# Weight loads in quarters, x tiles ahead of wk, k projections begun by block, single products for the factors, and engine orders written out, in a gated mix of segment attention and a token MLP

## The chip, the cores and the metric

The kernel runs on one core of a Trainium2 chip. The metric is device time in microseconds: the time of one execution of the program. Before the change three runs gave 178.17, 178.38 and 179.44, median 178.38.

## What is computed

Two branches work on the same x (2048 tokens by 448 features), and a gate per token mixes them. Cut to what matters:

```python
g = sigmoid((x * gate_w).sum(-1))
# A: 16 heads of 28 features; the sequence is cut into 4 segments of 512 tokens
q, k, v = x @ wq, x @ wk, x @ wv
for s in range(4):
    p = softmax(q_s k_s^T * 28**-0.5 + causal mask)          # inside the segment
    a_mem = phi(q_s) M / (phi(q_s) z + 1e-6)                 # what earlier segments left
    out_s = sigmoid(beta) * a_mem + (1 - sigmoid(beta)) * (p v_s)
    M, z = M + phi(k_s)^T v_s, z + phi(k_s).sum()            # phi(t) = t + 1 if t > 0 else exp(t)
a = out @ wo
# B: an MLP over the tokens (2048 -> 1792 -> 2048) for each feature
b = (gelu(layernorm(x)^T w1 + b1) w2 + b2)^T
return g * a + (1 - g) * b
```

## The kernel before, in words

Everything is one basic block. Each piece of work is recorded by `op` (line 89) with its engine, what it reads and writes, and an estimated cost; `plan` (line 157) then puts the recorded operations into one fixed order for each engine, and `finalize` (line 280) works out the semaphore waits. On the chip each engine runs its own list from the top, and an operation that waits holds up all that stand behind it on its engine. `plan` before the change is a list scheduler: it advances estimated times, takes for each engine the ready operation of the lowest priority number, shifts that number by a table (`SHIFTS`, line 354), and gives out PSUM banks and buffers as they come free. Where an operation names an `alt` engine, `plan` chooses between the two.

The stages are these.

- **Loading.** x comes in as 16 natural tiles of 128 tokens (`load_x`, line 522, into `xh`), and a second time as transposed tiles `xT` by DMA transposes from DRAM (`transpose_x`, line 536) for segments 1 to 3. Segment 0 is transposed on TensorE (`transposes_0`, line 667, matmuls of line 675) out of the first four x tiles. wk, wq and wv come in by `load_w` (line 526); VectorE then copies wk and wq into a padded layout `wqk` with 32 columns a head (`pad_w`, line 648, copies of line 649).
- **Projections.** q and k of a segment are made feature-major, v token-major. The 448 input features are 3 blocks of 128 and a remainder of 64, so `pair` (line 694) does two projections together: the two remainders as two 64-row tiles that run side by side (named lo...), then three full matmuls for each projection (pr...). For segment 0 the k projections are made in halves of 256 tokens. The last 4 features of each head's 32 rows hold parts of further heads; they are gathered through DRAM (`gather`, lines 755 and 760, DMAs on SP) into head group 3.
- **Attention.** 16 units (4 segments by 4 head groups) make 8 pairs of 5 fills. For each fill `scores` (line 942) does 4 row-tiled matmul groups into PSUM banks 0 to 3 (line 954), ScalarE takes one exp over 128x2048 (line 963), and GpSimd masks (line 966). `pv_unit` (line 971) multiplies by v with column tiles of 32 (line 990) and, from segment 1 on, by the memory (named mem). VectorE then transposes both results in 32x32 blocks (lines 1004, 1006), makes reciprocals and scales (1015 to 1019), GpSimd adds (1021), and VectorE transposes back into `oT` (line 1027), which the output projection `wo_tile` (line 1033) reads; ScalarE or VectorE takes that out (lines 1047, 1051). `do_mst` (line 831) accumulates the memory; four small products of 32 rows each (line 860) put it with the factor `maskg` into a block-diagonal matrix.
- **MLP.** `mm1` (line 1055) makes 14 tiles of 16 matmuls, `mm2` (line 1082) 16 tiles of 14 matmuls; their weights come through a ring of three slots of 1 MB (`ring_load`, line 569), one DMA and one semaphore for a slot. ScalarE and VectorE share the gelu (lines 1065 to 1078). VectorE finishes an output tile (line 1093) and SP stores it (line 1097). The last tile is done in columns 0 to 320 and 320 to 448.

All matmuls that may use any layout go through `mm` (line 329, matmul of line 332): as one 128x128 matmul, or, when the run of full-height work around them holds column-tiled ones, as four of 32 columns. So the TensorE stream alternates between four tile shapes: 128x128, 64 rows (lo), 32 rows (scores) and 32 columns.

Names that the text uses: `trx0_0` and `trx0_1` are the transposes of x tiles 0, 1 and 2, 3; `lok0_0` is the first remainder pair; `ot15` is the last transpose into `oT`; the wo tiles 12 to 15 read what `ot12` to `ot15` wrote, and are followed by the four last output tiles of `mm2`.

Of the kernel before, what the change touches and what calls it, by code (L numbers as in the profile page):

```python
# [74 lines left out]
class Sched:  # L75
# [13 lines left out]
    def op(self, eng, fn, reads=(), writes=(), name=None, dma=False, out=False, cost=100.0, prio=0.0, mode="f",  # L89
           nbytes=0, rel=0.0, port=False, take=None, use=(), alt=None,  # L90
# [27 lines left out]
        if dma:  # L118
            self._dma_uid += 1
            o.evspace = "dma_u%d" % self._dma_uid  # L120
            o.is_event = True
# [35 lines left out]
    def plan(self, shifts=()):  # L157

        import bisect

        shifts = dict(shifts)
        for o in self.ops:
            o.prio = (o.prio[0] + shifts.get(o.name.split("-")[0], 0.0), o.idx)
        succ = [[] for _ in self.ops]
        left = [0] * len(self.ops)
        ready = [o.rel for o in self.ops]
        for o in self.ops:
            for d in {x.idx: x for x in o.deps + o.order}.values():
                succ[d.idx].append(o)
                left[o.idx] += 1  # L170
        free = {e: 0.0 for e in ENGINES}
        mode = "f"
        chan = 0.0
        port = 0.0
        waiting = {e: [] for e in ENGINES}
        avail = {e: [] for e in ENGINES}
        banks = {p: {b: (0.0, []) for b in v} for p, v in self.pool.items()}
        for p, v in self.later.items():
            banks[p].update({b: (1e18, []) for b in v})

        def push(o):
            for e in o.alts:
                bisect.insort(waiting[e], (ready[o.idx], o.prio, o))

        for o in self.ops:
            if left[o.idx] == 0:
                push(o)
        line = []
        while len(line) < len(self.ops):
            best = None  # L190
            for e in ENGINES:
                w, a = waiting[e], avail[e]
                t = free[e]
                while w and w[0][0] <= t:
                    _, p, o = w.pop(0)
                    if o.start is None:
                        bisect.insort(a, (p, o))
                a[:] = [x for x in a if x[1].start is None]
                w[:] = [x for x in w if x[2].start is None]
                while True:  # L200
                    pick = None
                    can = [o for p, o in sorted(a + [(x[1], x[2]) for x in w if x[0] <= t])
                           if not o.take or sum(v[0] <= t for v in banks[o.take[0].pool].values()) >= len(o.take)]
                    if can:
                        pick = can[0]
                        if e == "PE":

                            if mode != "f":
                                lead = [o.prio for o in can if o.tile == "f"][:1]
                                tiled = [o for o in can if o.tile == "r" or o.tile == "h" and ([o.prio] <= lead or not lead)]  # L210
                                tiled = [o for o in tiled if o.tile == mode] + tiled
                                pick = tiled[0] if tiled else pick
                            elif pick.tile == "h":
                                rest = [o for o in can if o.tile == "f"]
                                if rest and not any(o.tile == "r" for o in can) and t < ready[pick.idx] + pick.hold:
                                    pick = rest[0]
                        break
                    nxt = [x[0] for x in w if x[0] > t][:1]
                    if a or w:
                        nxt += [v[0] for p in banks.values() for v in p.values() if t < v[0] < 1e12]  # L220
                    if not nxt:
                        break
                    t = min(nxt)
                if pick is not None and (best is None or t < best[0]):
                    best = (t, e, pick)
            t, e, o = best
            for g in o.take:
                pool = banks[g.pool]
                b = min((v[0], b) for b, v in pool.items())[1]
                g.bank = b  # L230
                o.deps = o.deps + pool[b][1]
                pool[b] = (1e18, [])
            o.eng = e
            o.fn, c, pt = o.alts[e]
            if o.evspace is None:
                o.evspace = e
            if e == "PE" and t < COLD:
                c *= 2.0
            if e == "PE" and o.tile != mode:
                c += SWITCH  # L240
                mode = o.tile
            if pt:
                t = max(t, port)
                port = t + c
            o.start = t
            o.cost = c
            free[e] = t + c
            if o.nbytes:
# [12 lines left out]
            for x in succ[o.idx]:  # L261
# [5 lines left out]
                if left[x.idx] == 0:  # L267
                    push(x)
# [955 lines left out]
```

## Time and profile before

| what | value |
|---|---|
| runs | 178.17, 178.38, 179.44 us, median 178.38 |
| profiled execution | 178.57 us, its span 176.8 us (1.77 us lie around it) |
| TensorE (PE) busy | 169.7 us, 2354 matmul records |
| VectorE (DVE) busy | 149.6 us, 337 instructions |
| ScalarE (ACT) busy | 134.1 us, 170 instructions |
| GpSimd (POOL) busy | 69.2 us, 93 instructions |
| granted TensorE clock | 1.0 throughout |

The page gives busy times by engine, the span in 40 slices, and the chain of work that ended last, followed back from the last instruction. The other views cut out a window, list instructions in order of time, group them by shape, or give each engine's busy time in chosen stretches. Matmuls are pipelined, so the time between the starts of matmuls, and not the busy time of one, is what a matmul costs.

### The profile page before, as it was taken

What the parts mean: (1) busy time and instruction counts of PE and PEld (TensorE: products, weight loads), DVE (VectorE), ACT (ScalarE), POOL (GpSimd) and SP (SyncE); (2) the same over time, 40 slices, a digit from 0 to 9 for tenths busy, and PEclk for the clock granted to TensorE, in tenths of its full rate; (3) what the DMA queues carried; (4) which work ended last, traced back from release to release, by engine and by line L of the source; (5) the groups of instructions that cost most, each with busy time, mean ns of one, the idle gap of its engine ahead of it and who ended that gap; (6) DMA issues with size and microseconds to landing.
All of it is one profiled execution on the core that took longest, in us unless ns stands there. A gap on an engine that the chain in (4) does not pass through costs nothing.

```text
span 176.8 us, 5552 instructions
## 1 busy us (share of the span) xinstructions
PE 169.7 (96%) x2354; PEld 81.8 (46%) x2354; DVE 149.6 (85%) x337; ACT 134.1 (76%) x170; POOL 69.2 (39%) x93
## 2 busy tenths in 40 slices
PE   8699999999999999999999999999999999999993
PEld 3343443345544544444544344444444544555652
DVE  6499999799995898998999999997889999992222
ACT  2277898999689999999999999987878877405100
POOL 8003016542302233437745644359474425450000
PEclk9999999999999999999999999999999999999999
DMA  6979983699939915852007360203938600166511
GB/s 153 281 142 304 259 158 84 167 302 193 245 78 268 240 35 161 192 171 46 4 11 201 77 170 22 61 28 95 224 99 227 170 8 4 56 176 194 153 59 52
DMA packets 49752, 24.62 MB, mean 139 GB/s; under 512 B 14256, under 2 KB 49488, under 8 KB 49728
## 3 DMA queue, kind: packets, MB, share of 16 engines
q1 hardware_dynamic: 49440, 24.05, 56.6%
q8 instruction: 18, 0.29, 0.7%
q10 hardware_dynamic: 288, 0.23, 0.6%
q14 instruction: 6, 0.05, 0.1%
HBM read 18.76 MB, written 2.36 MB: 119 GB/s over the span
## 4 chain that ended last, share of the span: by engine, by line
PE 78%; ACT 6%; DVE 6%; DMA 4%; SPq 3%; issue 2%
PE t L332 67%; PE t L954 6%; PE t L990 4%; DMA t<-in_A_wk_dram 3%; ACT t L963 2%; SPq L760 1%; SPq L755 1%; DVE t L913 1%; PE t L840 1%; DMA t<-spare_heads 1%; ACT t L1076 1%; ACT t L1065 1%; ACT t L1047 1%; DVE t L1071 1%; DVE t L1073 1%
## 5 line engine op out<-in xcount | busy, mean ns | idle before, releaser
L332 PE MATMUL t<-t 128*32 128x448 bf16 (+10 forms) x1620 | 145.8, 347 | 2.8 <-DVE t L649 1.7
L332 PEld LDWEIGHTS t<-t 128*32 128x32 bf16 (+2 forms) x1620 | 66.6, 97 | 68.6 <-issue 15.1
L963 ACT ACTIVATE t<-t 128x2048 bf16<-128x2048 f32 x40 | 76.2, 1904 | 6.3 <-PE t L954 6.1
L966 POOL TENSOR_SCALAR_AFFINE_SELECT t<-t 128x512 bf16<-128x512 bf16 x64 | 46.8, 732 | 58.2 <-ACT t L963 54.4
L1093 DVE SCALAR_TENSOR_TENSOR t<-t 128x448 bf16<-128x448 f32 (+2 forms) x17 | 10.9, 653 | 12.8 <-PE t L332 12.8
L1021 POOL TENSOR_TENSOR t<-t 128x448 bf16<-128x448 f32 x12 | 14.6, 1219 | 9.7 <-DVE t L1019 9.1
L1047 ACT ACTIVATE t<-t 128x448 bf16<-128x448 f32 x12 | 8.5, 732 | 10.3 <-PE t L332 10.1
L954 PE MATMUL t<-t 28*128 28x512 bf16 (+3 forms) x256 | 15.8, 301 | 0.3 <-DMA t<-spare_heads 0.3
L906 POOL TENSOR_TENSOR t<-t 128x4 f32<-128x4 f32 x4 | 4.5, 1130 | 20.9 <-DVE t L904 20.9
L1006 DVE STREAM_TRANSPOSE t<-t 128x512 f32<-128x512 f32 x16 | 11.2, 701 | 0.9 <-PE t L990 0.9
L990 PE MATMUL t<-t 128*32 128x256 bf16 (+3 forms) x256 | 11.5, 299 | 0.4 <-ACT t L816 0.4
L954 PEld LDWEIGHTS t<-t 28*128 28x128 bf16 x256 | 4.5, 92 | 14.1 <-ACT t L963 6.9
L1027 DVE STREAM_TRANSPOSE t<-t 128x512 bf16<-128x512 bf16 x16 | 10.9, 687 | 0.0
L1073 DVE SCALAR_TENSOR_TENSOR t<-t 128x448 f32<-128x448 f32 x14 | 8.8, 636 | 1.5 <-ACT t L1068 1.5
L1076 ACT ACTIVATE t<-t 128x448 f32<-128x448 f32 x14 | 8.5, 612 | 1.8 <-DVE t L1073 1.8
L1065 ACT ACTIVATE t<-t 128x448 f32<-128x448 f32 x14 | 9.3, 674 | 0.7 <-PE t L332 0.7
L1078 DVE SCALAR_TENSOR_TENSOR t<-t 128x448 bf16<-128x448 f32 x14 | 9.6, 695 | 0.0
L897 DVE BATCH_NORM_STATS2 t<-t 128x6 f32<-128x448 bf16 x16 | 9.4, 608 | 0.1
L1017 DVE SCALAR_TENSOR_TENSOR t<-t 128x448 f32<-128x448 f32 x12 | 9.2, 776 | 0.1
L990 PEld LDWEIGHTS t<-t 128*32 128x32 bf16 x256 | 6.9, 97 | 5.0 <-ACT t L816 0.7
L1004 DVE STREAM_TRANSPOSE t<-t 128x512 f32<-128x512 f32 x12 | 8.4, 698 | 0.4
L778 DVE SCALAR_TENSOR_TENSOR t<-t 128x512 bf16<-128x512 bf16 x12 | 8.4, 708 | 0.0
(69 smaller groups left out, 144.3 us busy)
## 6 DMA issues: line engine op xcount, KB each, us to landing
t<-in_B_w_dram SPq DMA_DIRECT2D x7, 1024.0 KB, 7.1
t<-in_B_w_dram SPq DMA_DIRECT2D x8, 896.0 KB, 5.3
out_dram<-t SPq DMA_DIRECT2D x15, 112.0 KB, 2.4
t<-in_A_x_dram SPq DMA_DIRECT2D x3, 448.0 KB, 4.8
t<-in_A_wo_dram SPq DMA_DIRECT2D x4, 98.0 KB
t<-in_A_wq_dram SPq DMA_DIRECT2D x1, 336.0 KB, 5.5
t<-in_A_wv_dram SPq DMA_DIRECT2D x1, 336.0 KB, 5.7
spare_heads<-t SPq DMA_DIRECT2D x8, 32.0 KB
```

Source lines behind the costliest of these rows:

```text
L332: last = e.matmul(out[q], w[:, q], x, skip_group_check=True, **kw)
L954: last = e.matmul(bank(hl)[:, c0 : c0 + w], kT[r, hg, s * 512 + j * 128 : s * 512 + j * 128 + 128], qT[r, hg, s * 512 + 128 * j : s * 512 ...
L963: op("ACT", lambda e: e.activation(pslot(g), ps[:, 0:4, :], ACT.Exp, scale=SCALE), reads=R_bank[0:4], writes=[g.res], take=g, name=f"exp{p ...
L966: op("POOL", lambda e, c0=c0: e.affine_select(pslot(g)[:, :, c0 : c0 + 128], pslot(g)[:, :, c0 : c0 + 128], pattern=[[0, 4], [1, 128]], co ...
L990: last = e.matmul(bank(cb)[32 * hl : 32 * hl + 32, 128 * j : 512], vaug[:, 4 * s + j, 32 * h : 32 * h + 32], pslot(P_fill[u // 2][f])[:, h ...
L1006: dv(lambda e: e.transpose(t2[:, 0, :], bank(cb)[:, 0:512]), [bres(cb)], [R_tt[tb][0]], "ta", 630, use=(cb,))
L1021: op("POOL", lambda e: e.tensor_tensor(o3, n3[0], n3[1], op=ALU.add), reads=R_tt[tb], writes=[R_ob[tb]], name=f"o{u}", cost=1280, port=Tru ...
L1027: dv(lambda e: e.transpose(oT[:, hg, s * 512 : s * 512 + 512], o), [R_ob[tb]], qres(hg, s), "ot", 635)
L1047: op("ACT", lambda e: e.activation(ag(T), bank(b)[:, 0:D], ACT.Identity, bias=b2g[:, T : T + 1], scale=gcol[:, T : T + 1]), **buse(b), rea ...
L1065: op("ACT", lambda e: e.activation(gg[:, q, :], bank(b)[:, 0:D], ACT.Square, bias=b1s[:, ft : ft + 1], scale=math.sqrt(GC)), **buse(b), re ...
L1073: op("DVE", lambda e: e.scalar_tensor_tensor(gg[:, q, :], gg[:, q, :], 1.0, vh[:, q, :], op0=ALU.add, op1=ALU.mult), reads=[R_gg[q], R_vh[ ...
L1093: op("DVE", lambda e: e.scalar_tensor_tensor(outst[:, p, c0:c1], bank(b)[:, 0 : c1 - c0], omg[:, T : T + 1], ag(T)[:, c0:c1], op0=ALU.mult ...
```

## The change

**Loads.** Each ring slot is loaded by four DMAs of 256 KB (the last of a w2 slot is half as large), each with its own resource, and the four parts of a slot have four semaphores, which successive loads of the part share. A matmul of `mm1` or `mm2` waits for its own quarter alone. x tiles 0 to 3 are loaded one by one, 0 and 2 from SP, 1 and 3 from ACT, ahead of wk. The gate weights and the two biases are issued from ACT instead of SP. The loads of wo and w1 no longer wait for wv.

**Projections.** The k projections of segment 0 are done over 512 tokens. Their first two blocks of 128 features (a new operation, `pra`) need only the first 256 rows of wk, so they stand ahead of the remainder pair. `do_x` copies all 128 rows into group 3 of both kT and qT, and the two GpSimd clears of these (952 ns each) go. One of seven warm-up matmuls goes. The copy out of segment 0's transposes may be on either engine.

**Factors.** The memory matrix is written by one product over 128x512 instead of four of 32 rows; its factor, and the column of 1 - sigmoid(beta), are made by four operations with constant masks that GpSimd builds at the start, instead of twelve; two VectorE clears (698 and 165 ns) go. The sum of line 1021 may be on VectorE.

**Orders.** `plan` no longer schedules. It takes the order of each engine, with bank and buffer numbers, from a table `ORDER`, and only checks that the order can run. The list of differences, cut to its core:

```diff
-    def plan(self, shifts=()):
...
+    def plan(self, order):
+        seen, ops = {}, {}
...
+        held = {(g.pool, g.bank): g for o in self.ops for g in o.free if g.bank is not None}
...
+                word, _, n = word.partition("*")
+                word, _, banks = word.partition("@")
...
+        while any(queue.values()):
+            n = len(line)
             for e in ENGINES:
...
+                while queue[e] and ready(*queue[e][0]):
+                    o, banks = queue[e].pop(0)
...
-    load_x("SP", 0, 1)
-    load_x("ACT", 1, 1)
+    for t in range(4):
+        load_x(("SP", "ACT")[t % 2], t, 1)
     load_w(wk_nat, WK, R_wk, "wk", P_wk)
-    load_x("SP", 2, 2)
...
+        for part in range(4):
+            t = slice(4 * part, min(4 * part + 4, NT if k < 7 else NFT))
...
+            op("SP", lambda e, dst=dst, src=src: e.dma_start(dst, src), writes=[R_slot[r][part]],
+               name=f"ldw1_{k}_{part}" if k < 7 else f"ldw2_{k - 7}_{part}", dma=True, cost=500, nbytes=82000 * n,
+               prio=(-2.5, -0.5)[k] if k < 2 else 0, space=f"dma_s{r}_{part}")
...
-    warm_up(7, "warm", -1)
+    warm_up(6, "warm", -1)
...
+        for P, b, cs, c, rows in parts:
+            if "first" in P:
+                def head(e, cols=False, P=P, b=b):
...
+                    for c in (0, 1):
+                        last = mm(e, bank(b)[:, 0 : P["n"]], P["w"](c, rows), P["x"](c, rows), cols, start=c == 0, stop=False)
...
+        if tc == 0:
+            P["first"] = R_xT[0] + [R_wkp[0], R_wkp[3]]
...
-        for hl in range(4):
-            q = slice(32 * hl, 32 * hl + 32)
-            op("DVE", lambda e, q=q: e.tensor_tensor(mst_sb[q, s, :, q], mst_f32[q, :, :], maskg[q, :, :], op=ALU.mult),
...
+        op("DVE", lambda e: e.tensor_tensor(mst_sb[:, s].rearrange("p g (l c) -> p g l c", l=4),
+                                            mst_f32[:, :, None, :].to_broadcast([128, NHG, 4, 32]), maskg[:, :, :, :],
+                                            op=ALU.mult),
...
+               alt=("DVE", lambda e: e.tensor_tensor(o3, n3[0], n3[1], op=ALU.add), 535))
...
-               reads=[R_slot[fb % NSL], R_x[st]], writes=[bres(b)], ...
+               reads=[R_slot[fb % NSL][st // 4], R_x[st]], writes=[bres(b)], ...
...
-    pairs(0, do_k(0, 0, 0, 256), do_k(0, 1, 0, 256), do_k(0, 2, 0, 256), do_k(0, 2, 256, 256),
-          do_k(0, 0, 256, 256), do_k(0, 1, 256, 256))
+    pairs(0, do_k(0, 0), do_k(0, 1), do_k(0, 2), do_x(0), do_q(0, 0), do_q(0, 1), do_q(0, 2, 0, 256), do_q(0, 2, 256, 256))
...
-    sch.plan(SHIFTS)
+    sch.plan(ORDER)
```

The first words of the table for TensorE and for SP (a name, `@` its banks, `*` a count of operations in sequence):

```
"PE": warm trx0_0 trx0_1@45 warm2 pra0_0 gtr@6 pra0_2 pra0_1 lok0_0 lok0_2 prk0_1 btr@7 prk0_0 prx0_3 prk0_2 loq0_0 ...
"SP": ldx0 ldx2 ldwk0@0 ldwk1 ldwq0@1 ldwqb ldwv0 ldwvb dtx1_0 dtx1_1 ldx4 ldx8 ldw1_0_3 ldx12 ldwo3 ldw1_1_3 dtx2_1
      dtx2_0 tk0_0 ldw1_0_0 ldw1_2_1 gq0_1 ldw1_1_0 ldw1_0_1 gk0_2 gq0_3 gk0_1 gk0_0 ldbeta gk0_3 ldw1_0_2 ldw1_2_3 ...
```

Between the two built programs these operations change their engine: 22 go from ScalarE to VectorE (among them five outputs of the wo tiles, four gelu halves of lines 1068 and 1071, nine q and k copies, two v copies and two copies of the first transposes), 11 from VectorE to ScalarE, and two sums of line 1021 from GpSimd to VectorE. VectorE has 332 operations recorded (337 before), ScalarE 162 with 7 DMA issues among them (171 with 2), SP 150 (109). TensorE changes its tile shape 103 times after the first matmul on wk, 121 times before.

More of the change, by code (lines that the diff above doesn't have):

```diff
@@ L277, in plan @@
                 run.append(o)
-        return max(o.end for o in line)
     def finalize(self):
@@ L516, in build_kernel @@
     R_vpe, R_mhalf, R_rstd, R_nmr = R("vpe", 4), R("mhalf"), R("rstd", 4), R("nmr", 4)
-    R_slot = R("slot", NSL)
+    R_slot = [R(f"slot{i}_", 4) for i in range(NSL)]
     xv = x2.rearrange("(t p) d -> p t d", p=128)
```

370 lines of the change are left out of this document (190 added, 180 removed), and 28 rows, old and new, of the table SHIFTS.

## Prediction

> **What bounds the kernel now.** I read the page first, then the busy time of each engine in chosen stretches, then the chain of work that ended last, and last the lists in order of time for the start and for the end of attention.
>
> ```profile
> span 176.8 us, 5552 instructions
> PE 169.7 (96%) x2354; PEld 81.8 (46%) x2354; DVE 149.6 (85%) x337; ACT 134.1 (76%) x170; POOL 69.2 (39%) x93
> DVE  6499999799995898998999999997889999992222
> ```
>
> TensorE is busy 96% of the span, so at first sight it alone is the bound. The row of VectorE says more: it is full until the last four slices and nearly empty in them. Its 85% is an average over two stages. The stretches show it, with busy time after each engine's name in the order PE, PEld, DVE, ACT, POOL:
>
> ```profile
> 0.00:24.20 24.20, 21.35 (x123) 9.49 (x123) 19.26 (x64) 14.90 (x33) 5.03 (x14) 1.00 0.96 219
> 7.25:24.20 16.95, 16.59 (x103) 7.54 (x103) 15.42 (x53) 13.02 (x31) 1.40 (x1) 1.00 1.06 223
> 24.20:60.00 35.80, 35.30 (x374) 16.08 (x376) 31.52 (x85) 32.25 (x42) 12.62 (x17) 1.00 0.88 190
> 60.00:120.00 60.00, 59.06 (x856) 27.59 (x849) 58.13 (x114) 58.51 (x68) 29.94 (x37) 1.00 0.38 99
> 120.00:159.70 39.70, 39.70 (x661) 19.90 (x663) 36.48 (x71) 25.56 (x26) 21.65 (x26) 1.00 0.48 120
> 0.00:159.70 159.70, 155.41 (x2002) 73.07 (x2006) 145.38 (x330) 131.21 (x166) 69.23 (x93) 1.00 0.60 143
> ```
>
> From 60 to 120 us VectorE is busy 58.13 of 60 us and TensorE 59.06: both are full. VectorE idles 14.3 us before 159.7 us, and 4.94 of these lie before 24.2 us. TensorE, once it has begun on wk at 7.25 us, idles 0.36, 0.50, 0.94 and 0 us in the four stretches, 1.8 us together. Now the two ends:
>
> ```profile
> 1.73 4.98 DMA t<-in_A_wk_dram
> 6.73 0.48 DVE t L649 x2
> 7.25 0.28 PE t L332 x2
> 7.54 0.55 PE t L675 x8
> 110.18 0.33 PE t L954 x8
> 110.51 2.57 PE t L332 x13
> 123.50 2.19 PE t L332 x11
> 174.06 0.35 DVE t L1093
> ```
>
> ```profile
> 158.36 1.29 DVE L1027 STREAM_TRANSPOSE t<-t 128x512 bf16<-128x512 bf16 x2
> ```
>
> The start is a transfer: the 224 KB of wk, third in SP's list, are issued at 1.73 us, land at 6.71, are padded on VectorE, and only at 7.25 does TensorE begin. The end is the last two transposes into `oT`, over at 159.65. The wo tiles 12 to 15 need them, and with the four output tiles behind them they take until 174.06, 14.41 us. So the end is the later of two things: TensorE's own stream, and VectorE's last transpose plus 14.4 us. Before the change the two nearly meet.
>
> **The change part by part.** The sum is made against the profiled execution, 178.57 us for a span of 176.8; it is 0.19 us above the median of the runs, 178.38. What lies around the span (1.77 us) and behind 174.06 (the last VectorE step and its store) stays: the last tile is still split at 320 columns.
>
> TensorE's stream. The chain gives its prices: 13 matmuls and a change of tile shape take 2.57 us, 11 and a change 2.19, so a 448-column matmul costs 0.19 us and a change 0.10; the 8 score matmuls run four abreast and stream 512 columns, 0.19 x 512/448 = 0.22, and their row says 0.33, so 0.11 there. I take 0.11. The built order has 103 changes of shape after the first wk matmul against 121: 18 x 0.11 = 2.0 us less. The second eight transposes (0.55 us with their weights, of which about 0.05 is a change already counted) no longer stand behind wk: 0.5 us less. The columns streamed are else the same; k projections over 512 columns are two halves put together. If no stall took the place of the 1.8 us above, the stream would end 2.0 + 0.5 + 1.8 = 4.3 us earlier, at 169.8.
>
> The start. x tiles 2 and 3 now go ahead, but the large part of wk is again the third DMA of SP, behind as many bytes (448 KB). Nearest rows:
>
> ```profile
> t<-in_A_x_dram SPq DMA_DIRECT2D x1, 224.0 KB, 5.1
> t<-in_A_x_dram SPq DMA_DIRECT2D x1, 112.0 KB, 2.7
> ```
>
> If it lands as a 112 KB tile did (2.7 us) the first k matmul could run at about 6.0, when the x copies are done; if it lands as the 224 KB of x (5.1 us), at 7.4. I take 7.25 as before, since the row of the same size in the same place is the nearest, and keep -1.25 and +0.15. What `pra` then gains is order only: 6 matmuls run while the rest of wk (issued one place later than the 224 KB) is padded. Five more DMA issues on ACT end near 4.3 us, ahead of its first copy (two of before show the price); they cost nothing unless wk came at the 6.0 bound.
>
> ```profile
> 0.78 0.39 ACTq L523 DMA_DIRECT2D t<-in_A_x_dram  x1
> 1.20 0.46 ACTq L532 DMA_DIRECT2D t<-in_A_wk_dram  x1
> ```
>
> One warm-up matmul less costs nothing: TensorE waits for wk anyway.
>
> VectorE's work up to the last transpose. Rows for its prices:
>
> ```profile
> L860 DVE TENSOR_TENSOR t<-t 32x128 bf16<-32x128 f32 x12 | 4.7, 394 | 0.2
> L803 DVE SCALAR_TENSOR_TENSOR t<-t 128x512 bf16<-128x512 bf16 x12 | 8.2, 682 | 0.0
> L776 DVE TENSOR_SCALAR t<-t 128x512 bf16<-128x512 bf16 x12 | 3.7, 311 | 0.1
> L888 DVE COPY t<-t 28x112 f32<-28x112 f32 x4 | 0.8, 208 | 0.1
> L892 DVE COPY t<-t 32x4 f32<-32x4 f32 x4 | 0.6, 159 | 0.1
> L616 DVE MEMSET t<- 128x768 uint32 x1 | 0.7, 698 | 0.1
> L789 DVE CAST t<-t 128x512 bf16<-128x512 f32 x5 | 3.4, 690 | 0.7 <-PE t L332 0.5
> L1071 DVE TENSOR_SCALAR t<-t 128x448 f32<-128x448 f32 x8 | 5.3, 672 | 0.5 <-ACT t L1065 0.5
> L1019 DVE TENSOR_TENSOR t<-t 128x448 f32<-128x448 f32 x12 | 8.4, 700 | 0.0
> ```
>
> Taken off: twelve small products (4.7 us) for three of 512 columns, a form that the trace lacks; bounds are 311 ns (one operand, fast) and 776 (the slowest scale), I take 682 as the nearest shape with two operands, so 4.7 - 2.0 = 2.7. The clears 0.9. The factors: some 1.6 us in twelve against one of 0.7 and three small ones of 0.16, so 0.4. One output step that now stands behind the last transpose, and a small one, 0.8. Together 4.8. Put on, net of what goes the other way before that point: five q and k copies at 0.69 (3.45) and a wider one (0.3), one v copy (0.6), two gelu halves (1.34), one copy of the first transposes (0.4), two sums of 0.70: 7.5. Net +2.7; the means overlap where instructions follow each other (two transposes took 1.29, their mean is near 0.69), and with the fast bound for the product it is +1.2. I take +2.0, so 147.4 us of work.
>
> VectorE's idle time. Before 24.2 us it waits for the same wk: 4.94 stays. After it, two bounds: as before, 9.4 us; or none. Nearest is the stretch in which it was not starved, 60 to 120: 1.87 of 60, or 3.1%. Before, 4.3 of the 9.4 us fell between 24 and 60 us, where attention stood still: the scores of line 954 waited for the gathered heads.
>
> ```profile
> 51.02 1.70 DMA t<-spare_heads
> 52.86 0.40 PE t L954 x8
> 149.12 0.33 PE t L954 x8
> ```
>
> By its order the change reaches these scores after some 40.4 us of TensorE work from the start on wk (columns at 0.19 us for 448, changes at 0.11), at 47.6 instead of 52.86, and SP's last gather for them stands behind a quarter that is freed at about 39, so it lands near 45. So I let VectorE idle 3.1% from 24.2 us on. Its last transpose ends at T with T = 147.4 + 4.94 + 0.031 x (T - 24.2), which gives 156.4 us, and the stream behind it ends at 156.4 + 14.4 = 170.8. That is later than TensorE's own 169.8, so VectorE decides: 3.25 us less, and 178.57 - 3.25 = 175.3 us.
>
> What costs nothing. GpSimd loses two clears of 952 ns and gains six small ones; it is busy 69.2 us. ScalarE loses 22 operations of about 0.65 us and takes 11. Three outputs of wo tiles 13 to 15 on VectorE (0.73 us each) fall after T, where 7 instructions are all its work. SP has 45 more issues of w1 and w2, 0.39 us each by the row below: 18 us, spread over the span; what they hold up is the second rival.
>
> **The rivals.** *TensorE alone paces.* If VectorE idles less than 3.1% or its new work is the +1.2, T falls to about 155.4 and TensorE's 169.8 counts: 178.57 - 4.3 = 174.3. With wk at its early bound, 1.25 less: 173.0. For it: TensorE then runs ahead of VectorE all the way, as between 60 and 120. Against it: four PSUM banks serve everything but the scores, so a late VectorE soon stops TensorE.
>
> *The quarters come late.* A quarter in SP's list waits for its part of the slot and for the gathers in front of it. Rows:
>
> ```profile
> t<-in_B_w_dram SPq DMA_DIRECT2D x7, 1024.0 KB, 7.1
> t<-in_A_x_dram SPq DMA_DIRECT2D x3, 448.0 KB, 4.8
> 13.82 0.39 SPq L576 DMA_DIRECT2D t<-in_B_w_dram  x1
> 25.96 3.37 SPq L755 DMA_DIRECT2D spare_heads<-t  x6
> ```
>
> The tightest place is the second quarter of w1's first block. It stands behind the first gather of q, which needs the x projection of segment 1, at about 21.7 us by TensorE's order; with the three issues up to it, it goes out at about 22.6, and the first MLP tile wants it after 20.2 us of TensorE work, at 27.5: 4.9 us. A load four times as large takes 7.1, one of 448 KB 4.8. If a quarter of 256 KB took 7.1 too, TensorE would wait 2.2 us there, and with it all behind: 175.3 + 2.2 = 177.5. It decides from 4.9 us on. Against it: fewer bytes land sooner in every pair of rows shown. The Trainium skill, DMA: Bandwidth & Descriptors, Rules for kernel authors, asks for 1 MiB or more per DMA where bandwidth counts, so it speaks against cutting these loads. By the fit that the same page gives (Anatomy of one DMA, for DMAs issued by software: 2.0 us and the bytes at 436 GB/s) a quarter would take an estimated 2.6 us and a whole load 4.4; by that estimate the quarters would be in time and the sum would stay. The trace's 7.1 for the whole load is far above this fit, so the bandwidth is shared here.
>
> *VectorE idles as before: slower.* If the 14.3 us of idle time are the attention chain's own (exp, mask, the product with v, the sums) and not TensorE's doing, then the 2.0 us of copies moved to VectorE are simply added: T = 159.65 + 2.0, the end 2.0 later, 180.6. It decides from an idle time of 12.3 us on (14.3 - 2.0): there the change gains nothing. For it: 5.1 of the 14.3 us fall after 60 us, and 3.2 of these between 120 and 159.7, when TensorE never waited. Against it: the same count of TensorE work puts attention's last scores, at 149.12 in the chain above, near 142, so VectorE's last units are fed 7 us earlier. The Trainium skill, TensorEngine Tiling (Array Packing), PSUM Bottleneck, warns that tiling speeds up TensorE and not the emptying of PSUM, which may become the bottleneck; it wants both ScalarE and VectorE used for that. The trace agrees that VectorE is full (58.13 of 60), and ScalarE has room after 120 us (25.56 of 39.70), so by that rule copies moved to VectorE late in the program are on the wrong engine.
>
> *The change does not do what it says* at the start: x ahead of wk leaves wk where it was. That is my base case, 0 us; it is no separate time.
>
> **How the numbers follow.** The forecast, VectorE paces and idles at 3.1%, gets 0.45; its own range is 174.5 (work +1.2) to 176.5 (work +2.7 and 0.5 us of waits on TensorE). TensorE alone, 173.0 to 174.3: 0.27. Late quarters, 177.5: 0.12. Idle as before, 180.6: 0.11. The rest, 0.05, is split evenly over waits that a new order may bring. A measurement of this kernel can tell about 1% from no change: 176.6 and 180.2 are the bounds. Faster by over 1%: 0.45 + 0.27 + 0.02 = 0.74; within 1%: 0.12 + 0.01 = 0.13; slower by over 1%: 0.13. The predicted time is the forecast's, 175.3. The range goes from 172.8, just under TensorE alone with an early wk, to 178.4, over the late quarters; it leaves out the idle-as-before case and tails, some 0.17.
>
> **What would show each step.** Start: the first 128x512 matmuls on wk at 7.25 (6.0 to 7.4), wk's landing before them. Stream: changes of shape still 0.10 to 0.11 in the chain. VectorE: the three products near 0.68 us, its busy time to the last transpose into `oT` near 147.4, that transpose at 156.4, idle 9.0. Gather: the third fill of the second pair at about 47.6 instead of 52.86. Quarters: landing under 4.9 us, no wait of line 264 (the new line of `mm`) for a w DMA. End: 14.4 us after T. The prediction is wrong if TensorE waits over 2 us for a weight quarter, or if VectorE's idle time before T is above 12 us, or under 7.

## The result, and the profile after

| | runs | median us | range us | ratio to the kernel before, 95% |
|---|---|---|---|---|
| before | 4 | 178.27 | 177.17 to 179.44 | |
| after | 4 | 176.05 | 174.92 to 177.61 | 0.9873 [0.9826, 0.9919] |
| after once more, beside the next three experiments | 12 | 176.56 | 175.07 to 178.03 | 0.9930 [0.9892, 0.9968] |

The change is faster. How much is less sure than either row alone says: the two intervals overlap only between 0.989 and 0.992, and the two ratios stand for 2.3 and 1.2 us. The medians here and below are of all executions, while the ratios leave out those that took over 1.5% more than the fastest of their kernel (one of the first four, two of the next twelve, four of the ten of *wk first* and one of the four of *heavy VectorE* further down). The forecast, 175.3 us, is below both medians, and its range, 172.8 to 178.4, holds every one of the 16 executions. The profile below is that of the slowest of the first four, 177.61 us; a profile of 175.07 us, from the repeat, stands beside it, because the difference between the two turns out to tell most.

The page of the changed kernel, in the places that were shown of the kernel before (busy time, VectorE in 40 slices), and the landing times of the weight quarters:

```profile
span 175.9 us, 5771 instructions
...
PE 169.1 (96%) x2441; PEld 83.4 (47%) x2441; DVE 149.6 (85%) x332; ACT 127.7 (73%) x156; POOL 64.5 (37%) x95
...
DVE  2699998588989997999899999999899969999114
...
t<-in_B_w_dram SPq DMA_DIRECT2D x52, 256.0 KB, 3.5
```

The shares of TensorE and VectorE are those of before, and they hide what has moved. The stretches (busy time behind each engine's name in the order PE, PEld, DVE, ACT, POOL) show it:

```profile
0.00:24.20 24.20, 22.95 (x122) 10.31 (x123) 19.19 (x63) 13.61 (x29) 4.24 (x17) 1.00 1.06 218
24.20:60.00 35.80, 34.70 (x437) 16.35 (x439) 30.89 (x81) 31.94 (x41) 12.61 (x18) 1.00 0.69 176
60.00:120.00 60.00, 59.13 (x854) 27.78 (x838) 56.69 (x107) 56.30 (x62) 27.98 (x36) 1.00 0.39 103
120.00:159.18 39.18, 37.99 (x710) 19.56 (x710) 36.03 (x75) 25.09 (x25) 19.65 (x25) 1.00 0.46 134
0.00:159.18 159.18, 154.77 (x2089) 74.00 (x2093) 142.80 (x321) 126.93 (x155) 64.48 (x95) 1.00 0.58 144
```

VectorE is less busy in three of the four stretches than in the same ones before (56.69 against 58.13 from 60 to 120), and up to its last transpose into `oT` it idles 159.18 - 142.80 = 16.4 us. TensorE idles 1.10, 0.87 and 1.19 us in the last three stretches, 3.2 us. The chain of waits shows the two largest, both put down here to DMAs:

```profile
1.71 5.38 DMA t<-in_A_wk_dram
7.64 0.60 PE t L264 x2
24.13 5.09 DMA t<-in_B_w_dram
29.27 2.25 PE t L264 x11
137.96 3.24 PE t L264 x68
141.20 1.19 issue
142.40 0.40 PE t L961 x8
173.56 0.35 DVE t L1101
```

The quarter issued at 24.13 is the second of w1's first block; the wait at 141.20 is that of scores `sc7_2` ("issue" because several semaphores are waited for and none is named). Of what these scores read, the gathered q of the last segment was issued last, at 138.8, so the wait is taken to be for it; its landing is not in the trace. The two lists in order of time show the end, VectorE first:

```profile
157.85 1.33 DVE L1035 STREAM_TRANSPOSE t<-t 128x512 bf16<-128x512 bf16 x2
154.75 18.76 PE L264 MATMUL t<-t 128*32 128x448 bf16 x448
49.40 0.40 PE L961 MATMUL t<-t 28*128 28x256 bf16 x8
```

From 154.75 to the end TensorE runs 448 matmuls in one piece: when it reaches the wo tiles, VectorE's transposes are there. The third row is the third fill of the second pair, at 49.40 instead of 52.86.

The profile of the execution that took 175.07 us, chain of waits and stretches:

```profile
1.73 4.22 DMA t<-in_A_wk_dram
6.50 0.61 PE t L264 x2
22.48 4.98 DMA t<-in_B_w_dram
27.51 2.25 PE t L264 x11
```

```profile
24.20:60.00 35.80, 35.32 (x482) 17.02 (x479) 32.02 (x78) 32.55 (x39) 13.86 (x20) 1.00 0.64 164
60.00:120.00 60.00, 58.79 (x785) 27.38 (x784) 56.85 (x106) 55.72 (x60) 27.09 (x35) 1.00 0.39 106
120.00:156.64 36.64, 36.64 (x701) 18.88 (x703) 34.69 (x72) 24.00 (x25) 18.88 (x24) 1.00 0.47 138
0.00:156.64 156.64, 153.95 (x2089) 73.59 (x2093) 143.80 (x321) 126.97 (x155) 64.05 (x95) 1.00 0.56 147
```

Here TensorE idles 0.48 and 1.21 us and then not at all, 1.7 us, as much as before the change, and VectorE 12.8 us up to T, the last transpose into `oT`. It is the same program, 2.54 us apart, and TensorE's two traces laid on each other differ in four places only: wk lands after 4.22 instead of 5.38 us, so TensorE starts 1.14 us earlier; the wait for the quarter is 0.62 us shorter; the one for the gather (1.26 us by the starts of matmuls) is absent; and a wait of 0.48 us for a VectorE gelu near 105 shows only in the faster one. 1.14 + 0.62 + 1.26 - 0.48 = 2.54. Between these places TensorE's shift stays the same within 0.06 us, and VectorE, with its own shifts here and there, has the same shift again behind each of them: it follows TensorE.

### The profile page after: what moved, and what is told of

Read it like the earlier page. It is cut to its first block, busy times and chain, and to the rows that moved or that the text cites. A ratio compares the mean times of both kernels' runs of the same rounds, so it can differ in the third digit from the quotient of the medians.

```text
span 175.9 us, 5771 instructions
## 1 busy us (share of the span) xinstructions
PE 169.1 (96%) x2441; PEld 83.4 (47%) x2441; DVE 149.6 (85%) x332; ACT 127.7 (73%) x156; POOL 64.5 (37%) x95
## 4 chain that ended last, share of the span: by engine, by line
PE 83%; DVE 6%; DMA 6%; ACT 1%; issue 1%; SPq 1%
PE t L264 71%; PE t L961 6%; PE t L997 5%; DMA t<-in_A_wk_dram 3%; DMA t<-in_B_w_dram 3%; DVE t L1081 1%; PE t L846 1%; ACT t L816 1%; DVE t L734 1%; DVE t L1035 1%; DVE t L779 1%; DVE t L781 1%; SPq L508 0%; DVE t L1059 0%; DVE t L1011 0%
## 5 line engine op out<-in xcount | busy, mean ns | idle before, releaser
L264 PE MATMUL t<-t 128*32 128x448 bf16 (+8 forms) x1708 | 144.5, 348 | 1.8 <-DMA t<-in_B_w_dram 1.1
L970 ACT ACTIVATE t<-t 128x2048 bf16<-128x2048 f32 x40 | 75.1, 1877 | 8.6 <-PE t L961 7.8
L973 POOL TENSOR_SCALAR_AFFINE_SELECT t<-t 128x512 bf16<-128x512 bf16 x64 | 45.6, 728 | 47.3 <-ACT t L970 46.4
L1028 POOL TENSOR_TENSOR t<-t 128x448 bf16<-128x448 f32 x10 | 12.1, 1211 | 24.7 <-DVE t L1024 8.6
L1055 ACT ACTIVATE t<-t 128x448 bf16<-128x448 f32 x9 | 6.4, 726 | 13.7 <-PE t L264 13.7
L997 PE MATMUL t<-t 128*32 128x512 bf16 (+3 forms) x256 | 11.5, 299 | 0.5 <-DVE t L1011 0.5
L1081 DVE SCALAR_TENSOR_TENSOR t<-t 128x448 f32<-128x448 f32 x14 | 9.1, 664 | 1.4 <-ACT t L1076 1.3
L1073 ACT ACTIVATE t<-t 128x448 f32<-128x448 f32 x14 | 8.9, 632 | 1.5 <-PE t L264 1.2
L781 DVE SCALAR_TENSOR_TENSOR t<-t 128x512 bf16<-128x512 bf16 x12 | 9.2, 764 | 0.0
L1086 DVE SCALAR_TENSOR_TENSOR t<-t 128x448 bf16<-128x448 f32 x14 | 9.0, 651 | 0.0
L806 DVE SCALAR_TENSOR_TENSOR t<-t 128x512 bf16<-128x512 bf16 x12 | 8.6, 722 | 0.0
L1024 DVE SCALAR_TENSOR_TENSOR t<-t 128x448 f32<-128x448 f32 x12 | 8.2, 682 | 0.1
```

What stands on the lines that cost most here:

```text
L264: last = e.matmul(out[q], w[:, q], x, skip_group_check=True, **kw)
L781: op("DVE", lambda e: e.scalar_tensor_tensor(kphi[:, p, :], ks, 0.0, kphi[:, p, :], op0=ALU.max, op1=ALU.add), reads=kres(hg, tc) + [R_kph ...
L970: op("ACT", lambda e: e.activation(pslot(g), ps[:, 0:4, :], ACT.Exp, scale=SCALE), reads=R_bank[0:4], writes=[g.res], take=g, name=f"exp{p ...
L973: op("POOL", lambda e, c0=c0: e.affine_select(pslot(g)[:, :, c0 : c0 + 128], pslot(g)[:, :, c0 : c0 + 128], pattern=[[0, 4], [1, 128]], co ...
L997: last = e.matmul(bank(cb)[32 * hl : 32 * hl + 32, 128 * j : 512], vaug[:, 4 * s + j, 32 * h : 32 * h + 32], pslot(P_fill[u // 2][f])[:, h ...
L1028: op("POOL", lambda e: e.tensor_tensor(o3, n3[0], n3[1], op=ALU.add), reads=R_tt[tb], writes=[R_ob[tb]], name=f"o{u}", cost=1280, port=Tru ...
```

## The experiments

Two theories. *VectorE decides*: the prediction's. *TensorE paces*: the end is TensorE's start, its stream and its waits, several of them for DMAs. In the table, start is the first matmul on wk, T the end of the last transpose into `oT`, both of the profiled execution; "start to end" goes from that matmul to the end of the span. Each ratio is to runs of the kernel before on the same chip.

| version | median us | ratio, 95% | start | T | start to end |
|---|---|---|---|---|---|
| before (first profile) | 178.27 | | 7.25 | 159.65 | 169.6 |
| before, second profile | 177.22 | 0.998 [0.994, 1.002] | 6.44 | 159.32 | 170.0 |
| after (first profile) | 176.05 | 0.987 [0.983, 0.992] | 7.64 | 159.18 | 168.3 |
| after once more | 176.56 | 0.993 [0.989, 0.997] | 6.50 | 156.64 | 166.9 |
| quarter ahead | 175.73 | 0.989 [0.984, 0.993] | 6.86 | 157.54 | 167.4 |
| gather ahead | 176.00 | 0.989 [0.985, 0.993] | 6.96 | 157.51 | 167.5 |
| both ahead | 175.53 | 0.988 [0.984, 0.992] | 7.08 | 158.02 | 167.7 |
| wk first | 177.04 | 0.992 [0.988, 0.996] | 8.40 | 158.71 | 167.0 |
| no column form | 179.01 | 1.008 [1.005, 1.010] | 6.93 | 159.93 | 169.7 |
| light VectorE | 175.13 | 0.987 [0.982, 0.992] | 7.12 | 156.69 | 166.3 |
| heavy VectorE | 180.19 | 1.013 [1.008, 1.019] | 6.55 | 161.20 | 171.1 |
| TensorE's order | 175.59 | 0.989 [0.983, 0.995] | 6.57 | 156.63 | 167.1 |
| all orders | 175.16 | 0.987 [0.982, 0.993] | 6.39 | 156.49 | 166.9 |
| whole loads | 203.67 | 1.147 [1.136, 1.157] | 7.04 | 178.98 | 196.0 |

**After once more.** No edit.

> The changed kernel once more, beside the next three. Both theories expect about 176.0 us and a ratio to the kernel before of 0.987; a profile of an execution near the median shows whether the two waits of TensorE in the first profile (1.17 us at 28.1 for a quarter of w1, 1.26 us at 141.2 for the gathered heads) belong to the kernel or to that execution, which at 177.6 was its slowest.

The ratio was 0.993, not 0.987, and the two waits are not a fixed cost: in an execution whose first loads land earlier, one is less than half as long and the other is gone.

**Quarter ahead, gather ahead, both.** SP's list:

```diff
-dtx2_0 tk0_0 ldw1_0_0 ldw1_2_1 gq0_1 ldw1_1_0 ldw1_0_1 gk0_2
+dtx2_0 tk0_0 ldw1_0_0 ldw1_0_1 ldw1_2_1 gq0_1 ldw1_1_0 gk0_2
```
```diff
-ldw2_3_1 ldw2_5_3 ldw2_5_2 ldw2_4_1 ldw2_4_0 out2 ldw2_3_2 gk3_h1 gk3_h0 gq3_3 gq3_1 gq3_2 gq3_0 ldw2_5_0
+ldw2_3_1 gk3_h1 gk3_h0 ldw2_5_3 ldw2_5_2 ldw2_4_1 ldw2_4_0 ldw2_3_2 gq3_3 gq3_1 gq3_2 gq3_0 out2 ldw2_5_0
```

> In SP's list the second quarter of w1's first block moves ahead of the first gather of q, so it goes out near 22.2 us instead of 24.13 and lands about 1.9 us earlier. Theory 'TensorE paces': the wait of 1.17 us at 28.1 goes and the end comes 1.0 to 1.2 us earlier than the changed kernel's. Theory 'VectorE decides': VectorE was busy all through that wait (1.40 of 1.40 us), so the last transpose into oT stays at 159.2, and the end moves by no more than the 0.5 us that lay between that transpose and the first wo tile: 0 to 0.5 us.

> In SP's list the gather of the last segment moves ahead of one output store, and its two k parts ahead of three w2 quarters, so the gathered q land about 1.1 us earlier. Theory 'TensorE paces': the wait of 1.26 us at 141.2 shrinks to 0 to 0.3 us, the end 0.9 to 1.2 us earlier. Theory 'VectorE decides': VectorE was busy through it (1.50 of 1.50 us from 141.0 to 142.5), so 0 to 0.5 us.

> Both moves. Theory 'TensorE paces': the gains add, 2.0 to 2.4 us, near 173.7 us. Theory 'VectorE decides': at most the 0.5 us once, near 175.5 us, with new idle time of TensorE behind late PSUM releases.

The medians lie 0.8, 0.6 and 1.0 us under the unchanged one, but the intervals overlap, and from start to end no profile of the three is shorter than the faster one of the unchanged kernel (167.4 to 167.7 against 166.9): no gain is shown, and the two do not add. The waits that were aimed at are gone (the second was already absent in the unchanged kernel's faster profile), but with the quarter ahead others come. TensorE's waits in the version with both moves:

```profile
PE t L264 <- DVE t L639: 1.0, 1, 1.0
...
PE t L997 <- DVE t L1011: 0.5, 1, 0.5
PE t L264 <- DMA t<-in_B_w_dram: 0.4, 1, 0.4
...
PE t L961 <- ACT t L970: 0.3, 1, 0.3
PE t L846 <- issue: 0.2, 1, 0.2
```

Lines 264, 961 and 846 wait here at 49, 53 and 60 us for another quarter, for an exp that stood behind a late transpose of phi, and for that segment's memory transposes: 0.9 us between 49 and 60 that the unchanged version hardly has. Up to 24 us the DMA share is 1.06 in the first profile after, all 16 DMA engines busy, so what goes ahead in SP's list may well push back what it passes. The spread tells more than the medians: the slowest of the 18 executions of these three versions took 176.63 us, while 6 of the 12 unchanged ones took 176.8 or more.

**wk first.** `ldx0 ldx2 ldwk0 ldwk1` becomes `ldwk0 ldx0 ldx2 ldwk1`.

> The large part of wk moves from third to first in SP's list, ahead of x tiles 0 and 2. In the five profiles of this chip's work so far TensorE began on wk between 6.50 and 7.64 us (mean 7.01), 0.55 us behind wk's landing, and the copies of x were done near 6.0. Theory 'TensorE paces from its start': it begins near 6.2 and the time falls by the difference, 0.5 to 0.9 us from the changed kernel's median of 176.56. Theory 'VectorE decides': VectorE waits for the same wk, so it also gains 0.5 to 0.9. Rival: the landing is set by the bytes of all first loads together, wk lands at 5.9 to 7.1 as before, no change.

Neither theory had this: it starts later, at 8.40. Chain of waits:

```profile
1.31 3.23 DMA t<-in_A_x_dram
4.58 1.89 PE t L665 x16
6.47 2.13 PE t L628 x5
8.61 0.85 PE t L264 x2
```

wk now lands at 3.9, but x at 4.54, and x has the longer way: 16 transposes, then copies. TensorE stands for 1.04 us ahead of the transposes and still works at half its pace behind them: five warm-up matmuls of 512 columns take 2.13 us, 0.43 each, against 1.25 us, 0.25 each, in the profile of 175.07 us, where the transposes follow the first warm-up at once. The list in order of time of that profile, and below it the same five matmuls in the first profile after:

```profile
3.57 1.69 PE L665 MATMUL t<-t 128*128 128x128 bf16 x16
5.10 1.25 PE L628 MATMUL t<-const-bfloat16-1.0 128*128 128x512 bf16 x5
```

```profile
5.24 2.02 PE L628 MATMUL t<-const-bfloat16-1.0 128*128 128x512 bf16 x5
```

The first warm-up matmuls lie 0.43 us apart in every profile, so each program starts at half pace. The gap need not be what prolonged it here: in the first profile after, TensorE worked from 0.82 us on without a gap of more than 0.1 us and was still at half pace until 6.8 us. Over the other profiles the half pace ends anywhere from 3.7 us on; here it lasts until about 10, the latest of all, and why is open. The Trainium skill, TensorE: Matmul & The Clock Gate, Part 1, says that the array runs at half its clock until it has been busy for about 3.4 us; the halving agrees with the durations, the 3.4 us do not fit the first profile after (6.0 us of work at half pace), and the granted clock in the views says 1.00 throughout. In this one profile x ahead of wk gives the earlier start; in time the two orders can't be told apart (0.992 against 0.993). That this version's start to end is no longer than the others' (167.0) says that the time lost stays lost at the start.

**No column form.** `x.cols = x.mode == "x" and any(...)` becomes `x.cols = False`.

> No 128x128 matmul is cut into four of 32 columns any more, so TensorE changes its tile shape 139 times instead of 103; nothing else changes. Theory 'TensorE paces, a change costs 0.11 us': 36 x 0.11 = 4.0 us more, near 180.5. Theory 'VectorE decides': TensorE may run up to some 2 us later without moving the end, so 0 to 2 us more. If a change of shape costs nothing by itself, 0.

From start to end 169.7 against 166.9: 2.9 us for 36 changes of shape, 0.08 each; by the medians 2.5. That is more than the other theory allowed and less than 36 x 0.11. The waits do not explain why it is less. The 0.5 us for line 997 is gone, but others are longer:

```profile
6.93:159.93 153.00, 150.48 (x1335) 66.68 (x1349) 140.50 (x314) 125.45 (x153) 62.29 (x80) 1.00 0.55 141
```

TensorE idles 2.5 us up to T here, against 1.7 in the profile of 175.07 us. That leaves 2.1 us for the 36 changes, 0.06 each, while the starts of two matmuls still lie about 0.1 us further apart across a change (0.285 us from a 128x128 of 448 columns to a score, 0.189 between two of the former). Where the rest of it goes is open.

**Light and heavy VectorE.** One leaves out the 24 `scalar_tensor_tensor` that finish phi; the other does the minimum of phi twice (shown for q, the same for k):

```diff
-        op("DVE", lambda e: e.tensor_scalar_min(ph, ph, 1.0), ...
+        for _ in range(2):
+            op("DVE", lambda e: e.tensor_scalar_min(ph, ph, 1.0), ...
```

> Leaves out the 24 VectorE operations of 128x512 that finish phi of k and q (max with 0 and add), so phi is only exp capped at 1: 24 x 0.6 to 0.7 us = 14 to 17 us less VectorE work. Theory 'TensorE paces': only the waits of TensorE for VectorE can go (0.73 us near 77, 0.33 near 80, twice 0.33 near 99, 0.5 near 105: 2.2 us together), so 0.5 to 2.2 us less, 174.3 to 176.0. Theory 'VectorE decides at 3.1% idle': the end falls to TensorE's own bound, by the prediction's sum 1.0 us or more below the changed kernel. This run alone bounds what VectorE costs; the next one tells the theories apart.

> Each of the 24 minimum operations of phi is done twice, with the same output: 24 x 0.2 to 0.31 us = 5 to 7 us more VectorE work, spread from 15 to 155 us. Theory 'VectorE decides': the last transpose into oT comes 5 to 7 us later less what little idle time there is, the end 4 to 7 us later, 180.5 to 183.5. Theory 'TensorE paces, VectorE has 12.8 us of idle time before its last transpose': most of it disappears in idle time, 0 to 2 us more.

The stretch up to T, first the light, then the heavy version:

```profile
0.00:156.69 156.69, 153.29 (x2080) 73.84 (x2093) 129.26 (x297) 126.61 (x155) 62.06 (x95) 1.00 0.57 147
```

```profile
0.00:161.20 161.20, 154.06 (x2088) 72.72 (x2097) 152.89 (x345) 127.02 (x155) 65.23 (x95) 1.00 0.55 143
```

14.5 us less VectorE work than in the profile of 175.07 us (143.80 - 129.26) bring 1.4 us of the median, with intervals that overlap, and 0.6 us from start to end; T comes no earlier than in that profile (156.69 against 156.64, with a start 0.6 us later). So T follows TensorE and not VectorE's work: VectorE does not decide in the changed kernel. But more was added than expected, 9.1 us and not 5 to 7, and it cost 4.3 us from start to end, more than the 2 that 'TensorE paces' allowed and inside the other theory's 4 to 7. VectorE's idle time falls from 12.8 to 8.3 us: about 4.5 us of the addition went into it, the rest lengthened the kernel. Only this one size was tried, so whether 4.5 us alone would have been free is not shown, nor what the 8.3 us that are left belong to. In the heavy version TensorE waits for VectorE in several places; its largest rows:

```profile
PE t L264 <- DVE t L1081: 1.1, 1, 1.1
PE t L264 <- DVE t L1103: 1.0, 1, 1.0
...
PE t L264 <- DVE t L1013: 0.8, 1, 0.8
```

So TensorE paces, with VectorE as the next bound, which decides by the time that 9 us are added to it. The Trainium skill, TensorEngine Tiling (Array Packing), PSUM Bottleneck, names the emptying of PSUM as what may hold a tiled TensorE back. The three steps in these rows read PSUM, so the heavy version agrees, with 2.9 us; in the profile of 175.07 us all waits for VectorE behind the start come to 1.2 us.

**The kernel before once more.** No edit.

> The kernel before, with a second profile of it. It shows whether its start on wk (7.25 us in its first profile) spreads as that of the changed kernel does (6.50 to 7.64), and whether its stream from the start on (169.56 us from the first matmul on wk to the end) stays. Theory 'the start is no gain, the changes of tile shape are': start within 6.5 to 7.6, and start to end 169.0 to 170.0, some 2 to 2.7 us more than the changed kernel's 166.9 to 167.7. Rival 'the earlier x tiles gain at the start': start at 7.2 or later.

The chain of its second profile:

```profile
2.17 4.70 DMA t<-in_A_x_dram
6.92 0.62 PE t L675 x8
```

Start 6.44, inside the spread of the changed kernel, so no gain of the start on wk is shown; but the second eight transposes then waited for x tiles 2 and 3, issued behind wk, until 6.92. From start to end it took 170.0 us, 2.4 to 3.2 us more than the four profiles of the first batch and 1.8 more than the first profile after: the gain lies in the stream.

**TensorE's order, and all orders.**

```diff
-u10-4 pv5@4 u10-5*2 u11-1 u10-7 u11-2 u10-8 sc3_2
+u10-4 u10-5*2 u11-1 u10-7 pv5@4 u11-2 u10-8 sc3_2
-wo5@5 y2-0@6*6 pv8@4 y0-0@5 sc5_1
+wo5@5 pv8@4 y2-0@6*6 y0-0@5 sc5_1
```

> Two moves in TensorE's list alone: the product with v of unit 5 goes four MLP matmuls later, that of unit 8 six earlier; the work of every engine stays. TensorE waited 0.71 us ahead of the first (for a VectorE transpose out of its PSUM bank) and 0.53 us ahead of the matmul that now follows the second (for a VectorE gelu). Theory 'TensorE paces': both waits go, 0.9 to 1.2 us less than the changed kernel, ratio near 0.986. Theory 'VectorE decides': the products come at another time but VectorE has the same work, 0 to 0.3 us.

> The two moves in TensorE's list and the two in SP's list (second quarter of w1's first block, gather of the last segment) together. Theory 'TensorE paces': 1.2 us less than the version with SP's two moves alone (ratio 0.988 to the kernel before), so a ratio near 0.981, 174.3 us. Theory 'VectorE decides': 0.988 again.

With TensorE's moves alone the median is 1.0 us under the unchanged one, as expected, but the intervals overlap, and from start to end the profile is no shorter (167.1 against 166.9); added to SP's moves they bring 0.4 more, not 1.2. Waits in the version with all moves:

```profile
PE t L997 <- POOL t L973: 0.3, 1, 0.3
PE t L961 <- ACT t L970: 0.3, 1, 0.3
PE t L264 <- DVE t L1079: 0.3, 1, 0.3
PE t L264 <- DMA t<-in_B_w_dram: 0.2, 1, 0.2
```

Line 997 no longer waits 0.5 us for VectorE but 0.3 for a mask of GpSimd, and GpSimd, ScalarE, VectorE and a quarter each hold TensorE up once, for 0.2 to 0.3 us. This version has the lowest median but one, 175.16 us, and of the versions that compute the whole function the lowest; its interval overlaps that of the unchanged kernel.

**Whole loads.** Four DMAs and four semaphores a slot become one, issued when the slot is free; TensorE's list stays.

> Each ring slot is loaded by one DMA again, issued as soon as the slot's last reader is through by the profile of the changed kernel (the first three at the place of their first quarter); TensorE's list stays as it is. By that profile TensorE's first matmul on block 3 of the ring comes 0.75 us behind the last reader of the slot, that on block 4 with it, those on blocks 13 and 14 5.7 and 4.7 us behind. With 7.1 us for a whole load, theory 'this order lives from the quarters': waits of 6.3, 7.1, 1.4 and 2.4 us, 10 to 17 us more, 186 to 193. Rival 'a quarter is as good as a whole load': under 2 us more.

203.67 us, beyond the 186 to 193 expected. Waits, and four stretches:

```profile
PE t L264 <- DMA t<-in_B_w_dram: 13.3, 3, 6.0
PE t L264 <- DMA t<-in_A_x_dram: 2.2, 1, 2.2
```

```profile
43.00:49.00 6.00, 0.85 (x5) 0.29 (x3) 4.26 (x12) 1.73 (x3) 0.36 (x1) 0.98 0.88 217
49.00:60.00 11.00, 10.82 (x129) 4.66 (x128) 5.56 (x11) 7.58 (x10) 2.18 (x3) 0.85 0.19 26
60.00:66.00 6.00, 0.22 (x1) 0.13 (x2) 3.53 (x7) 2.83 (x3) 1.68 (x2) 0.71 0.77 197
66.00:75.00 9.00, 9.00 (x103) 4.05 (x105) 3.39 (x8) 4.00 (x5) 0.64 (x1) 0.82 0.01 2
```

The waits are where they were expected (blocks 3 and 4 of the ring, some 6 us each), and behind each the granted clock (the number behind the five engines) is lower, 0.85 and 0.82 as means of these stretches. In narrower ones it is 0.50 from 49.2 to 52 us and from 66 to 69, and 1.00 again from 55 and from 72 on; behind the wait for x near 27 us and behind the last one near 187 it is 0.50 too. Some 15 us of work ran so, at half the clock, which by an estimate from these stretches is 7 to 8 of the 27 us lost: a wait of TensorE costs a second time, and the expectation had left that out. With whole loads this order of TensorE is 27 us longer; whether another order would suit them was not tried. The rule of the Trainium skill, DMA: Bandwidth & Descriptors, Rules for kernel authors, to move 1 MiB or more per DMA, is given for bandwidth. It is no guide here: a quarter is there after 3.5 us, a whole load after 6.1, and what TensorE needs next is the first quarter.

## Why the prediction was right in its number and wrong in its mechanism

The predicted time and its range held. The step "VectorE decides" did not: by the prediction's own condition (idle time of VectorE ahead of T above 12 us) it is refuted, with 16.4 and 12.8 us. What happened is nearest to the rival *TensorE alone paces*, but TensorE came 3.4 us (first profile) and 2.0 us (faster profile) later than that rival had it for the measured starts, so that the time came out near the forecast for another reason. That agreement is luck. Point by point:

- **Start, base 7.25, bounds 6.0 to 7.4.** Measured 6.39 to 7.64 in the eleven profiles whose first loads are in this order. The nearest row gave the middle well; that one program starts over 1 us apart from one execution to the next, and that the whole time follows, was not foreseen. No gain at the start, as forecast.
- **Changes of shape and transposes, 2.0 + 0.5 us.** From the start to the last VectorE step, with its waits up to T taken off, TensorE needs 162.8 us in both profiles after, against 165.0 and 164.2 in the two before: 1.4 to 2.2 us less. So this part of the sum is about right and is most of the measured gain of 1.2 to 2.3. How it divides is not shown: by the version without column form a change is worth 0.06 to 0.08 us to the end, so 18 of them an estimated 1.0 to 1.4 us.
- **Transposes ahead of wk, 0.5 us of these.** Not tried alone. The second profile of the kernel before shows them waiting until 6.92 behind a start at 6.44, so there is something to gain.
- **TensorE's waits, 1.8 us that could vanish: the failed term of TensorE's sum.** By the same stretches they are 3.2 us in the first profile after, and 1.7 us in the faster one (1.8 and 3.1 in the two before). A removed wait came back as others, and the quarters and gathers in SP's list, each a little late, are among them. These waits are nearly all of the 3.4 and 2.0 us by which TensorE came later than the rival had it.
- **VectorE's work, +2.0 us: the failed term of VectorE's sum.** Busy time to T went from 145.38 to 142.80 and 143.80, 1.6 to 2.6 us less. The products were as forecast (0.677 us each). Of the moved operations, each counted with what it adds to the busy time, the two gelu halves, the v copy and the two sums came to +3.0 us against 3.3, and the q and k copies to +2.6 against 3.75: two of the five added copies have 256 columns (0.42 us) and were priced as 512. With the savings, all that the sum counted comes to about +1.1. The other 2.7 us and more lie in instructions that both kernels have in the same number, which the sum took as unchanged. An example, before and in the profile of 175.07 us:

```profile
L1017 DVE SCALAR_TENSOR_TENSOR t<-t 128x448 f32<-128x448 f32 x12 | 9.2, 776 | 0.1
```

```profile
L1024 DVE SCALAR_TENSOR_TENSOR t<-t 128x448 f32<-128x448 f32 x12 | 8.2, 682 | 0.1
```

The twelve products behind these went from 700 to 619 ns (line 1019, now 1026) and the four scales of the first segment from 842 to 701 (line 1025, now 1033); the second profile of the kernel before has the old times. Why they are shorter is open. The sum's lower bound, +1.2, does not follow from its rows either: with the fast bound for the products they give +1.6. With 143.8 and the idle time of the heavy version, 8.3, VectorE alone would by this estimate have been through at 152.1, 4.5 us ahead of where it was; the forecast's idle time of 9.0 was not put to the test.
- **T at 156.4.** Measured 156.64 in the faster profile: 143.8 of work and 12.8 of idle time instead of 147.4 and 9.0. A number that agrees for the wrong reason.
- **Gather, 47.6 instead of 52.86.** 49.40 in the first profile after, 47.64 in the faster one; the gathered heads did not hold it up. But the gather of the last segment probably did, in the first profile, and no step of the prediction looked there.
- **Quarters.** The place named as the tightest was the one where TensorE waited: 1.10 us in one profile, 0.48 in the other, against 2.2 us in the rival. The quarter took 5.1 and 5.0 us there, between the 4.9 that it could take and the 7.1 of the rival; the median quarter takes 3.5. So the sign "no wait of line 264 for a w DMA" failed. That fewer bytes land sooner in every pair of rows was not so in the prediction's own rows: 224 KB took 5.1 us, 448 KB 4.8.
- **The end, 14.4 us behind T.** 14.4 us in both profiles (173.56 - 159.18 and 171.02 - 156.64): the tail of TensorE's list is as long as it was, though T no longer releases it.
- **What lies behind the last VectorE step** was to stay. It is 2.75 and 2.74 us to the end of the span in the two profiles before and 2.3 to 2.6 in those after (*whole loads* apart): 0.1 to 0.4 us of the gain that no step had.
- **The rival 'VectorE idles as before'** fails: with 9.1 us more work its idle time falls to 8.3 us, so at least 4.5 us of it was not the attention chain's own.

What stays open: how the gain splits between the changes of shape and the earlier transposes, what the quarters alone would do in the order of before (not tried), why VectorE's unchanged instructions take less, and why wk's landing varies between 4.0 and 5.4 us with the same loads ahead of it.

## What to carry to other kernels

Where two engines are nearly full, compute for each the time at which it could be through alone, and bound the idle time by an experiment that adds work: here 14.5 us less of VectorE work gained 1.4 at most, which says that it does not pace, and 9.1 more cost 4.3, which says that it is not far from it. A wait that an edit removes is rarely all gain: look in the order for what is late next, on each queue, and count a list of tight DMAs as a spread of times and not as a fixed cost. Before a load goes ahead, follow what has to happen between its landing and its use; the one with the longest way goes first.

## What was not expected of the hardware

- The same 224 KB, third in SP's list, landed after 4.0 to 5.4 us in eleven profiles with the same loads ahead of it (4.22 and 5.38 in the two of the same program); first in the list it took 3.14.
- TensorE began every program at 0.43 us for 512 columns and went over to 0.22 at a time that varies from 3.7 to 6.8 us with the same loads, and near 10 in *wk first*; the granted clock in the views reads 1.00 all the while.
- Behind or within waits of TensorE of some 6 us, and of 2.2 us once, the granted clock fell to 0.50 for 3.4 to 6.8 us.
